# Batch 0 of a block-mixed attention: half of the queries selected early, keys alone on 128 partitions, last values behind the keys

## The chip, the cores and the metric

The kernel runs on one core of a Trainium2 chip. The metric is device time in microseconds (us). The kernel before takes 249.59 us, the median of three runs that lie between 249.53 and 250.57 us.

## The reference

Two steps follow each other. The first is an attention in blocks: batch 4, 8 heads, 768 positions, head size 64, 8 blocks of 96 positions. An 8x8 matrix per head (`sort_net`) goes through five rounds of exponent, row sums and column sums, and then mixes the blocks of keys and of values; each block of queries sees only its own mixed block. The second step is a gated feed-forward on the 3072 tokens of 512 features, with 1536 hidden columns.

```python
P = sort_net
for _ in range(5):
    P = np.exp(P - np.max(P, axis=-1, keepdims=True))
    P = P / (np.sum(P, axis=-1, keepdims=True) + 1e-09)
    P = P / (np.sum(P, axis=-2, keepdims=True) + 1e-09)
k_sb = np.einsum('bhij,bhjcd->bhicd', P, k_b)      # k_b, v_b: (4, 8, 8 blocks, 96, 64)
v_sb = np.einsum('bhij,bhjcd->bhicd', P, v_b)
scores = np.matmul(q_b, k_sb.transpose(0, 1, 2, 4, 3)) / np.sqrt(64)
attn = softmax(scores)
x = np.matmul(attn, v_sb)                          # to (3072 tokens, 512)
g = x @ w_gate                                     # (3072, 1536)
out = (g / (1 + np.exp(-g)) * (x @ w_val)) @ w_out
```

## The kernel before

**Stages.** A prelude computes the mixing weights of all batches on 32 partitions (one per batch and head), five rounds on VectorE with the exponent on ScalarE, while the inputs of batch 0 land. Then the blocks of batch 0 are mixed, the first half of its attention is done (units u = 0 to 3), and the feed-forward begins. It runs in eight pieces `ffn(0)` to `ffn(7)`, each for half a batch (384 tokens); in each, `gate(n, m)` and `value(n, m)` go over the 12 column blocks m of 128. The attention of what comes next is woven between these by hand: `merge` takes a list of feed-forward steps with a rough cost and places side steps at due times on that scale.

**Mixing on TensorE.** A tile of batch 0 holds queries and keys together: `load_q` puts the queries on partitions 64 to 127 (head, block) and `load_k` the keys on 0 to 63, 96 positions of 64 features on each. `kq_chunk(b, at, n, ...)` takes positions at to at+n; for each, two matmuls (`two`, the even and the odd heads) have the tile's slice as weights and `rmix` as the moving operand, 64 columns. `rmix[0]` has the mixing weights on the key rows and an identity on the query rows, so one pass mixes the keys, selects the queries, and puts both with features on partitions. A copy (`drain`) on VectorE ("v") or ScalarE ("s") moves each chunk out of PSUM into `kqt`. `v_chunk` mixes the values: they were first transposed within a partition into `vch` by `copy_v`, partly on GpSimd and partly on ScalarE, and one matmul per feature makes `vt`. A unit is four blocks of one head pair: `qk` (scores and exponent), `av` (values, division into `st`), `xtr` (transposes into `xts`). The four units of the first half each fill one 128-row part of `xts`, which are the four contraction steps of the feed-forward; `early` begins it before all four are there.

**Order.** TensorE, VectorE, ScalarE and GpSimd run in the order written until the first gate outputs; from there TensorE and GpSimd do. `fill` and `dots` are matmuls on zeros that keep TensorE occupied in known gaps.

**Loads.** All input loads are issued by GpSimd on one queue, in this order: values of batch 0 in two halves, queries, keys in four pieces; then GpSimd does its share of `copy_v`, and a one-element copy `landed` (L144), which reads the last key, holds GpSimd until all keys are in. Only behind it come the weights of gate and value, in pieces of 256 columns, with the values of batch 1 among them:

```python
    for m in range(0, 1024, 256):
        load_gv(m, m + 256)          # gate, then value weights, 256 columns each
    load_v(1, 0, C)
    for m in range(1024, DF, 256):
        load_gv(m, m + 256)
```

Column block m of `value` needs the piece that holds columns 128 m to 128 m + 127. PSUM is divided into tags: "gen" (three banks in turn), "a" and "b" (two banks each, one buffer), and "x" (one bank).

Of the kernel before, what the change touches and what calls it, by code (L numbers as in the profile page):

```python
# [17 lines left out]
def kernel(  # L18
# [72 lines left out]
    def load_k(b, lo, hi):  # L91
        rows = highr if b else lowr
        nc.gpsimd.dma_start(out=kq_tile(b)[rows, lo:hi, :], in_=k_nat[b, :, lo:hi, :])
# [6 lines left out]
    def load_q(b, lo, hi):  # L100
        rows = lowr if b else highr
        nc.gpsimd.dma_start(out=kq_tile(b)[rows, lo:hi, :], in_=q_nat[b, :, lo:hi, :])
# [30 lines left out]
    HC = C // 2  # L133
    load_v(0, 0, HC)
    load_v(0, HC, C)
    make_identity(nc, ident)
    load_q(0, 0, C)
    for lo, hi in ((0, 32), (32, 64), (64, 80), (80, 96)):
        load_k(0, lo, hi)
    copy_v(nc.gpsimd, 0, lowr, 0)  # L140
    copy_v(nc.gpsimd, 0, lowr, 3)
    copy_v(nc.gpsimd, 0, lowr, 5, 8, 40, D)
    landed = const.tile([R, 1], BF16)
    nc.gpsimd.tensor_copy(landed, kq_tiles[0][0:R, C - 1, D - 1:D])  # L144
    for m in range(0, 1024, 256):
        load_gv(m, m + 256)
    load_v(1, 0, C)
    for m in range(1024, DF, 256):
        load_gv(m, m + 256)
# [5 lines left out]
    for t in rmix.values():  # L155
        nc.vector.memset(t, 0.0)
# [13 lines left out]
    mask = const.tile([128, H], BF16)  # L170
    id4 = ident.rearrange("p (u h j) -> p h u j", u=2, h=H)
# [9 lines left out]

    p_ps = bank_tile("p_ps")[0:BH, 0:NB * NB].rearrange("p (i j) -> p i j", j=NB)
    for it in range(N_ITER):
        nc.scalar.activation(p_ps, p_sb if it == 0 else p_ps, AF.Exp)
        if it == 1:
            with nc.allow_low_precision("0/1 mask"):
                nc.vector.tensor_reduce(mask, id4, axis=AX.XY, op=ALU.add)
            nc.vector.tensor_copy(rmix[0][highr, 1].rearrange("p h i -> p (h i)"), ident[highr, highr])
        if it == 2:
            copy_v(nc.scalar, 0, lowr, 2, 8)  # L190
        if it == 3:
            copy_v(nc.scalar, 0, lowr, 3, 8)
        rowred = rowreds[it]
        nc.vector.reduce_sum(rowred[:, :, 0], p_ps, axis=AX.X)
        nc.vector.reciprocal(rowred, rowred)
        nc.vector.tensor_mul(p_ps, p_ps, rowred.to_broadcast([BH, NB, NB]))
        nc.vector.reduce_sum(colred[:, 0, :], p_ps.transpose([0, 2, 1]), axis=AX.X)
        nc.vector.reciprocal(colred, colred)
        if it < N_ITER - 1:
            nc.vector.tensor_mul(p_ps, p_ps, colred.to_broadcast([BH, NB, NB]))  # L200
    for lo in (0, NB // 2):
        part = slice(lo, lo + NB // 2)
        nc.vector.tensor_tensor(
            p_bf[:, part], p_ps[:, part].unsqueeze(2).to_broadcast([BH, NB // 2, H, NB]),
            colred.unsqueeze(1).to_broadcast([BH, NB // 2, H, NB]), op=ALU.mult)
    copy_v(nc.scalar, 0, lowr, 4, 8)
    copy_v(nc.scalar, 0, lowr, 5, 8, 0, 40)
# [30 lines left out]
    def v_chunk(b, at, n, eng, tag):  # L238
        rows = slice(0, 128) if b % 2 else lowr
        dst = vt_tile(b // 2)[:, b % 2]  # L240
        mix = rmix[b][rows, 0].rearrange("p a b -> p (a b)")
        tp = chunk_tile("tv", n // 8, tag).rearrange("p (l n) -> p l n", n=H * NB)
        for ld in range(n):
            col = (at + ld) * C
            nc.tensor.matmul(tp[:, ld, :], lhsT=vch[rows, col:col + 128], rhs=mix,  # L245
                             start=True, stop=True)
        drain(eng, dst[:, :, at:at + n], tp[0:C].transpose([0, 2, 1]))

    def v_pair_chunk(pair, at, n, eng, tag):
        dst = vt_tile(pair)[:, :, :, at:at + n]  # L250
# [8 lines left out]

    es, sts, xts = {}, {}, {}  # L260
    ecount = [0]

    def scores(b, u, tag):
        half, g = divmod(u, H2)
# [8 lines left out]
        for i4 in range(4):  # L273
            at = (g * NB + half * 4 + i4) * C
            for two in range(2):
                lo = two * D
                nc.tensor.matmul(pss[two][:, i4 * C:(i4 + 1) * C],  # L277
                                 lhsT=k_sb[lo:lo + D, k_at + at:k_at + at + 128],
                                 rhs=q_sb[lo:lo + D, q_at + at:q_at + at + C],
                                 start=True, stop=True)  # L280
# [15 lines left out]
    def av(b, u, tag="a"):  # L296
        half, g = divmod(u, H2)
# [3 lines left out]
        for two in range(2):  # L301
            e = es[(b, u)][two]
            for i4 in range(4):
                nc.tensor.matmul(o[:, two, i4, :], lhsT=e[:, i4 * C:i4 * C + 128],  # L304
                                 rhs=vt[:, 2 * g + two, half * 4 + i4, :],
                                 start=True, stop=True)
# [105 lines left out]
    idle_ps = bank_tile("idle_ps", "x")  # L412

    def fill(tile, n):
        for _ in range(n):
            nc.tensor.matmul(tile, lhsT=warm_sb[:, 0:128], rhs=warm_sb, start=True, stop=True)  # L416

    def dots(n):
        for _ in range(n):
            nc.tensor.matmul(idle_ps[0:32, 0:32], lhsT=warm_sb[:, 0:32], rhs=warm_sb[:, 0:32],  # L420
                             start=True, stop=True)

    dots(124)
    for it, n in ((1, 3), (2, 4), (3, 4), (4, 4)):
        nc.tensor.matmul(idle_ps[0:NB, 0:NB], lhsT=rowreds[it][:, :, 0], rhs=rowreds[it][:, :, 0],
                         start=True, stop=True)
        fill(idle_ps, n)

    def weights(half):
        w_ps = bank_tile(f"w_ps{half}")[:, 0:NB * B * H].rearrange("p (i b h) -> p i b h", b=B, h=H)  # L430
        for i in range(NB):
            nc.tensor.matmul(w_ps[half * R:(half + 1) * R, i].rearrange("p b h -> p (b h)"),
                             lhsT=p_bf[:, i].rearrange("p a b -> p (a b)"),
                             rhs=ident[0:BH, 0:BH], start=True, stop=True)
        return w_ps

    def mix_of(dst, b, w):
        lo = (b % 2) * R
        nc.vector.tensor_tensor(dst, mask[lo:lo + R].unsqueeze(2).to_broadcast([R, H, NB]),
                                w[lo:lo + R].transpose([0, 2, 1]), op=ALU.mult)  # L440

    w_lo = weights(0)
    mix_of(rmix[0][lowr, 0], 0, w_lo[:, :, 0])
    w_hi = weights(1)
    w_sb = const.tile([128, NB, 2, H], FP32)
    nc.scalar.copy(w_sb[lowr, :, 1], w_lo[lowr, :, 2])
    nc.scalar.copy(w_sb[highr], w_hi[highr].rearrange("p i (pair u) h -> p i pair u h", u=2)[:, :, :, 1])
    fill(idle_ps, 1)
# [4 lines left out]
    v_chunk(0, 48, 8, "v", "gen")  # L453
    v_chunk(0, 56, 8, "s", "gen")
    kq_chunk(0, 0, 8, "v", "gen")
    kq_chunk(0, 8, 16, "s", "a")
    kq_chunk(0, 24, 16, "v", "b")
    kq_chunk(0, 40, 8, "s", "gen")
    kq_chunk(0, 48, 8, "s", "gen")
    fill(idle_ps, 1)  # L460
    kq_chunk(0, 56, 16, "v", "a")
    fill(idle_ps, 1)
    kq_chunk(0, 72, 16, "s", "b")
    kq_chunk(0, 88, 8, "v", "gen")
    for b in range(1, B):
        rows = highr if b % 2 else lowr
        mix_of(rmix["p"][rows, b % 2] if b > 1 else rmix[1][rows, 0], b, w_sb[:, :, b // 2])
    fill(idle_ps, 4)
    qk(0, 0, "a")
    qk(0, 1, "b")  # L470
    qk(0, 2, "gen")
    idle_ps = bank_tile("idle_ps")
    fill(idle_ps, 2)
    av(0, 0, "a")
    fill(idle_ps, 2)
    av(0, 1, "b")
    fill(idle_ps, 1)
    xts[(0, 0)] = xtp.tile([128, H2, TW], BF16, name="xt0_0", tag="xt")
    qk(0, 3, "gen")
    av(0, 2, "a")  # L480
    x01 = xt_tile("x", 2)
    x_to(x01[:, 0], 0, 0)
    x_to(x01[:, 1], 0, 1)
    drain("s", xts[(0, 0)][:, 0:2, :], x01.rearrange("p g a b -> p g (a b)"))
    fill(idle_ps, 1)
    av(0, 3, "b")
    x2 = xt_tile("gen", 1)
    x_to(x2[:, 0], 0, 2)
    drain("s", xts[(0, 0)][:, 2:3, :], x2.rearrange("p g a b -> p g (a b)"))
    first = {}  # L490

    def early(n, kcs):
        sb, m, name = ((wg_sb, 0, "g_ps"), (wv_sb, 0, "v_ps"), (wg_sb, 1, "g_ps"))[n]
        if n not in first:
            first[n] = psum.tile([128, TW], FP32, name=name, tag="gen", bufs=3)
        for kc in kcs:
            nc.tensor.matmul(first[n], lhsT=sb[:, kc, ts(m, 128)], rhs=xts[(0, 0)][:, kc, :],
                             start=(kc == 0), stop=(kc == NKC - 1))

    early(0, (0, 1))  # L500
    early(1, (0, 1))
    x3 = xt_tile("x", 1)
    x_to(x3[:, 0], 0, 3)
    drain("v", xts[(0, 0)][:, 3:4, :], x3.rearrange("p g a b -> p g (a b)"))
    early(0, (2,))
    early(1, (2,))
    early(2, (0,))
    early(0, (3,))
    early(1, (3,))
    early(2, (1, 2, 3))  # L510
# [70 lines left out]
    merge(ffn(0), units(0, range(4, 8), (0.0, 5.6)))  # L581
# [47 lines left out]
```

## Time and profile before

| | us |
|---|---|
| median of three runs | 249.59 |
| the runs | 249.53, 249.59, 250.57 |
| span of the profiled execution | 248.0 |
| TensorE busy in it | 240.1 (97%) |
| VectorE, ScalarE, GpSimd busy | 157.7, 110.3, 52.5 |
| granted TensorE clock | 1.00 throughout |

The profiled execution's own time is given by its span alone, from its first to its last instruction; no separate time is listed for it. The median of the runs is 1.59 us above the span, and that is taken for what lies around it. TensorE's busy time includes the zero matmuls of `fill` and `dots`, and a matmul's end is modelled.

### The profile page before, as it was taken

What the parts mean: (1) busy time and instruction counts of PE and PEld (TensorE: products, weight loads), DVE (VectorE), ACT (ScalarE), POOL (GpSimd) and SP (SyncE); (2) the same over time, 40 slices, a digit from 0 to 9 for tenths busy, and PEclk for the clock granted to TensorE, in tenths of its full rate; (3) what the DMA queues carried; (4) which work ended last, traced back from release to release, by engine and by line L of the source; (5) the groups of instructions that cost most, each with busy time, mean ns of one, the idle gap of its engine ahead of it and who ended that gap; (6) DMA issues with size and microseconds to landing.
All of it is one profiled execution on the core that took longest, in us unless ns stands there. A gap on an engine that the chain in (4) does not pass through costs nothing.

```text
span 248.0 us, 6193 instructions
## 1 busy us (share of the span) xinstructions
PE 240.1 (97%) x2636; PEld 141.3 (57%) x2636; DVE 157.7 (64%) x332; ACT 110.3 (44%) x187; POOL 52.5 (21%) x47
## 2 busy tenths in 40 slices
PE   7899999999999999999999999999999999999994
PEld 6376566666555556655555655565555555555543
DVE  6778689887555775857657646755764585446700
ACT  2977553453544444454642552354244334232311
POOL 7948459960059200000000000000000000000000
PEclk9999999999999999999999999999999999999999
DMA  5959999999999296010122121112111121100122
GB/s 101 211 95 166 215 189 228 194 226 211 221 170 192 53 210 164 3 42 3 45 54 52 57 62 34 44 42 78 32 42 45 39 57 55 42 22 24 42 81 88
DMA packets 39530, 24.38 MB, mean 98 GB/s; under 512 B 27728, under 2 KB 35664, under 8 KB 38992
## 3 DMA queue, kind: packets, MB, share of 16 engines
q0 software_dynamic: 21328, 14.16, 38.9%
q1 hardware_dynamic: 18176, 9.84, 14.1%
q8 instruction: 20, 0.33, 0.5%
q14 instruction: 6, 0.05, 0.1%
HBM read 28.32 MB, written 7.86 MB: 146 GB/s over the span
## 4 chain that ended last, share of the span: by engine, by line
PE 83%; DVE 7%; ACT 3%; issue 3%; DMA 2%; DVEq 0%; ACTq 0%; POOLq 0%
PE v_ps L373 23%; PE o_ps L390 23%; PE g_ps L355 22%; PE tkq L233 4%; PE av_ps L304 3%; PE qk L277 2%; DVE gs_sb L365 2%; DMA v<-in_v_dram 2%; DVE st L310 2%; PE tv L245 2%; PE idle_ps L416 1%; DVE h L378 1%; PE o_ps L406 1%; ACT th_sb L363 1%; PE x_ps L321 1%
## 5 line engine op out<-in xcount | busy, mean ns | idle before, releaser
L365 DVE SCALAR_TENSOR_TENSOR gs_sb<-th_sb,g_ps 128x384 bf16<-128x384 bf16 x96 | 52.8, 550 | 51.8 <-ACT th_sb L363 49.1
L373 PE MATMUL v_ps<-xt,wv_sb 128*128 128x384 bf16 x380 | 77.3, 326 | 0.7 <-DVE gs_sb L365 0.4
L355 PE MATMUL g_ps<-xt,wg_sb 128*128 128x384 bf16 x376 | 76.5, 326 | 0.0
L363 ACT ACTIVATE th_sb<-g_ps 128x384 bf16<-128x384 f32 x96 | 47.1, 490 | 56.0 <-PE g_ps L355 53.5
L390 PE MATMUL o_ps<-wo_sb,h 128*128 128x512 bf16 x276 | 64.0, 379 | 0.0
L378 DVE SCALAR_TENSOR_TENSOR h<-v_ps,gs_sb 128x384 bf16<-128x384 f32 x96 | 53.3, 556 | 6.6
L373 PEld LDWEIGHTS <-wv_sb 128*128 128x128 bf16 x380 | 35.4, 97 | 24.6 <-issue 2.3
L355 PEld LDWEIGHTS <-wg_sb 128*128 128x128 bf16 x376 | 34.6, 97 | 23.2 <-issue 0.3
L390 PEld LDWEIGHTS <-h 128*128 128x128 bf16 x276 | 26.3, 98 | 28.9
L395 ACT COPY o_sb<-o_ps 128x512 f32<-128x512 f32 x23 | 13.5, 585 | 50.8 <-PE o_ps L390 50.8
L124 POOL COPY vch<-v 64x1536 bf16<-64x1536 bf16 (+2 forms) x11 | 28.6, 2639 | 20.7 <-DMA v<-in_v_dram 20.7
L290 ACT ACTIVATE e_all<-qk 96x768 bf16<-96x768 f32 x30 | 22.6, 802 | 8.1 <-PE qk L277 8.1
L310 DVE TENSOR_TENSOR st<-av_ps,r_sb 96x512 bf16<-96x512 f32 x32 | 21.7, 679 | 0.2
L304 PEld LDWEIGHTS <-e_all 96*128 96x128 bf16 x256 | 12.2, 98 | 4.9 <-ACT e_all L290 0.8
L304 PE MATMUL av_ps<-vt,e_all 96*128 96x65 bf16 x256 | 13.5, 194 | 0.0
L211 DVE CAST vt<-tv 96x1024 bf16<-96x1024 f32 (+1 forms) x9 | 9.8, 1100 | 2.7 <-PE tv L255 1.6
L308 DVE RECIPROCAL r_sb<-av_ps 96x8 f32<-96x8 f32 x32 | 6.4, 199 | 7.6 <-PE av_ps L304 7.5
L213 ACT CAST vt<-tv 96x1024 bf16<-96x1024 f32 (+1 forms) x9 | 9.2, 1032 | 3.1 <-PE tv L255 1.8
L211 DVE CAST kqt<-tkq 128x1024 bf16<-128x1024 f32 (+1 forms) x7 | 7.5, 1068 | 2.7 <-PE tkq L233 2.6
L213 ACT CAST kqt<-tkq 128x1024 bf16<-128x1024 f32 (+1 forms) x7 | 6.0, 894 | 6.6 <-PE tkq L233 6.6
L416 PE MATMUL idle_ps<-warm_sb 128*128 128x512 bf16 x28 | 8.7, 409 | 0.0
L233 PE MATMUL tkq<-rmix,kq 128*64 128x64 bf16 x384 | 7.8, 197 | 0.6 <-issue 0.6
(74 smaller groups left out, 126.3 us busy)
## 6 DMA issues: line engine op xcount, KB each, us to landing
out_dram<-o_sb SPq DMA_DIRECT2D x23, 256.0 KB, 2.0
v<-in_v_dram POOLq DMA_DIRECT2D x3, 768.0 KB, 19.9
kq<-in_q_dram POOLq DMA_DIRECT2D x2, 768.0 KB, 13.6
wg_sb<-in_moe_w_gate_dram POOLq DMA_DIRECT2D x6, 256.0 KB, 8.5
wv_sb<-in_moe_w_val_dram POOLq DMA_DIRECT2D x6, 256.0 KB, 9.1
wo_sb<-in_moe_w_out_dram POOLq DMA_DIRECT2D x1, 1536.0 KB, 23.8
kp<-in_k_dram POOLq DMA_DIRECT2D x2, 768.0 KB, 15.1
q_scr<-in_q_dram POOLq DMA_DIRECT2D x2, 768.0 KB, 29.9
```

Of the source, the lines that this page charges most:

```text
L124: eng.tensor_copy(dst, src.transpose([0, 2, 1]))
L211: nc.vector.tensor_copy(dst, src)
L233: nc.tensor.matmul(tp[two * D:(two + 1) * D, lc, :], lhsT=kq_tiles[b][:, at + lc, :], rhs=rm[:, two], start=True, stop=True)
L290: nc.scalar.activation(e_all[:, n:n + 2, 0:4 * C], wide[0:C, :, 0:4 * C], AF.Exp, scale=scale)
L304: nc.tensor.matmul(o[:, two, i4, :], lhsT=e[:, i4 * C:i4 * C + 128], rhs=vt[:, 2 * g + two, half * 4 + i4, :], start=True, stop=True)
L310: nc.vector.tensor_tensor(st.rearrange("p i two d -> p two i d"), o[0:C, :, :, 0:D], r_sb.to_broadcast([C, 2, 4, D]), op=ALU.mult)
L355: nc.tensor.matmul(g_ps, lhsT=wg_sb[:, kc, ts(m, 128)], rhs=xt[:, kc, :], start=(kc == 0), stop=(kc == NKC - 1))
L363: nc.scalar.activation(th_sb, g_ps, AF.Tanh, scale=0.5)
L365: nc.vector.scalar_tensor_tensor(gs_sb, th_sb, 1.0, g_ps, op0=ALU.add, op1=ALU.mult)
L373: nc.tensor.matmul(v_ps, lhsT=wv_sb[:, kc, ts(m, 128)], rhs=xt[:, kc, :], start=(kc == 0), stop=(kc == NKC - 1))
L378: nc.vector.scalar_tensor_tensor(h_tiles[n][:, m, :], v_ps, 0.5, gs_tiles.pop(m), op0=ALU.mult, op1=ALU.mult)
L390: nc.tensor.matmul(o_ps, lhsT=h_w[:, m, ts(t3, 128)], rhs=wo_sb[:, m, :], start=(m == 0), stop=(m == NFC - 1))
```

## The change

The tile of batch 0 becomes `qk0`: keys on all 128 partitions for 48 positions (the first 48 positions of each block on 0 to 63, the last 48 on 64 to 127), and the queries in two quarters of the tile, `q0[0]` and `q0[1]`, one for each half of the sequence. A half is 16 runs of 24 rows, and its partitions are (run, head) with the run outermost. `q0_chunk` selects the first half with the identity ahead of the mixing weights, in the fifth round; the second half, `q0_rest`, is the first side step of `ffn(0)`. `k0_chunk` mixes the keys alone, with a block-diagonal `rmix[0]` that one instruction makes. The last 16 features of the values are mixed behind the keys. Units 0 to 3 of batch 0 are cut differently (two head pairs by two blocks), so that `early` can begin with half of the tokens. The division of `copy_v` over GpSimd and ScalarE changes, the second query half is loaded behind the first weights, the weights from column 512 on come in pieces of 512 columns, and units 4 to 7 are due later in `ffn(0)`.

```diff
+    q_runs = q.rearrange("b h (t r c) d -> b t r h (c d)", t=2, c=QC)          # QC = 24, HC = 48
+    qk0 = natp.tile([128, C, D], BF16, name="qk0", tag="nat")
+    q0 = [qk0[:, HC + t * QC:HC + (t + 1) * QC, :] for t in range(2)]
+    k0 = qk0[:, 0:HC, :]
+    def load_q0(t):
+        nc.gpsimd.dma_start(out=q0[t].rearrange("p c d -> p (c d)"), in_=q_runs[0, t])
     load_v(0, 0, HC)
     load_v(0, HC, C)
     make_identity(nc, ident)
-    load_q(0, 0, C)
-    for lo, hi in ((0, 32), (32, 64), (64, 80), (80, 96)):
-        load_k(0, lo, hi)
-    copy_v(nc.gpsimd, 0, lowr, 0)
-    copy_v(nc.gpsimd, 0, lowr, 3)
-    copy_v(nc.gpsimd, 0, lowr, 5, 8, 40, D)
-    nc.gpsimd.tensor_copy(landed, kq_tiles[0][0:R, C - 1, D - 1:D])
-    for m in range(0, 1024, 256):
-        load_gv(m, m + 256)
+    load_q0(0)
+    for a, rows in enumerate(halves):
+        nc.gpsimd.dma_start(out=k0[rows], in_=k_nat[0, :, a * HC:(a + 1) * HC, :])
+    copy_v0(nc.gpsimd, 0, QC, 0, D3)               # positions, features; D3 = 48
+    copy_v0(nc.gpsimd, HC, C, 0, D3 // 2)
+    copy_v0(nc.gpsimd, HC, C, D3 // 2, D3)
+    copy_v0(nc.gpsimd, HC, C, D3, D)
+    nc.gpsimd.tensor_copy(landed, k0[:, HC - 1, D - 1:D])
+    load_gv(0, 256)
+    load_q0(1)
+    load_gv(256, 512)
+    load_gv(512, 1024)
     load_v(1, 0, C)
-    for m in range(1024, DF, 256):
-        load_gv(m, m + 256)
+    load_gv(1024, DF)
...
+        if 1 < it < 4:
+            copy_v0(nc.scalar, QC + (it - 2) * QC // 2, QC + (it - 1) * QC // 2)
+        if it == 4:
+            early_q = [q0_chunk(0, 0, 16, "b"), q0_chunk(0, 16, 8, "gen")]
+            for dst, src in early_q:
+                drain("s", dst, src)
+            copy_v0(nc.scalar, 0, QC, D3, D)
...
+            fill(idle_ps, (3, 4, 4, 1)[it - 1])    # was 3, 4, 4, 4
...
-    v_chunk(0, 48, 8, "v", "gen")
-    v_chunk(0, 56, 8, "s", "gen")
-    kq_chunk(0, 0, 8, "v", "gen")
...
+    k0_chunk(0, 8, "v", "gen")
+    k0_chunk(8, 8, "s", "gen")
+    k0_chunk(16, 8, "v", "gen")
+    k0_chunk(24, 16, "s", "a")
+    k0_chunk(40, 8, "v", "gen")
+    v_chunk(0, 48, 16, "v", "b")
     fill(idle_ps, 2)
...
+    mix_of(3)
+    x_first(0, "v", "x")                           # 4 transposes, copied out: all features of 2 blocks
+    av(0, 2, "a")
+    x_first(1, "s", "x")
+    early(0, range(NKC), 0)                        # 192 tokens at a time
+    av(0, 3, "b")
+    early(1, range(NKC), 0)
+    x_first(2, "s", "x")
+    early(2, range(NKC), 0)
+    x_first(3, "v", "x")
+    for n in range(3):
+        early(n, range(NKC), 1)
...
-    merge(ffn(0), units(0, range(4, 8), (0.0, 5.6)))
+    def q0_rest():
+        for at, n, eng, tag in ((0, 16, "s", "b"), (16, 8, "v", "a")):
+            drain(eng, *q0_chunk(1, at, n, tag))
+    merge(ffn(0), [(0.0, q0_rest)] + units(0, range(4, 8), (2.0, 6.6)))
```

In the new order `w_ps`, the transposed mixing weights, stays in the "x" bank until `mix_of(3)` has read it, and `x_first` uses the same bank.

## The prediction

> **What bounds the kernel now.** I read the page's busy times first, then the chain of waits in order of time, then the timelines of GpSimd and TensorE, and last the DMA issues with their times to landing. The page says that TensorE is what the time is made of:
>
> ```profile
> PE 240.1 (97%) x2636; PEld 141.3 (57%) x2636; DVE 157.7 (64%) x332; ACT 110.3 (44%) x187; POOL 52.5 (21%) x47
> ```
>
> So a change to the prelude can win in only one way: the feed-forward's matmuls start earlier and then run without a gap. The chain (start, duration, what) gives the fixed points:
>
> ```profile
> 11.28 0.29 PE w_ps L432 x4
> ...
> 20.31 0.62 PE qk L277 x24
> ...
> 27.41 0.65 PE v_ps L373 x4
> ```
>
> The mixing weights start at 11.28, the first scores at 20.31, and 27.41 is the first steady feed-forward step, value(0,1). The prelude is a chain of copies out of PSUM and waits, padded with zero matmuls; from 27.41 on TensorE is dense. Behind it stands the weight queue, in GpSimd's timeline (start, duration, engine, line, what):
>
> ```profile
> 6.30 6.18 POOL L124 COPY vch<-v 64x1536 bf16<-64x1536 bf16 x3 [0.70 <-DMA v<-in_v_dram]
> 15.94 0.18 POOL L144 COPY landed<-kq 64x1 bf16<-64x1 bf16 x1 [3.45 <-DMA kq<-in_k_dram]
> 16.06 0.80 POOL L111 DMA_DIRECT2D wg_sb<-in_moe_w_gate_dram  x1
> ```
>
> GpSimd ends its copies at 12.48, waits for the keys until 15.94, and only then issues weights. In the DMA issues (the last figure is the us from issue to landing) the first piece of gate weights, the first of value weights (issued 16.84) and the last (issued 27.25) stand as
>
> ```profile
> wg_sb<-in_moe_w_gate_dram POOLq DMA_DIRECT2D x1, 256.0 KB, 3.8
> wv_sb<-in_moe_w_val_dram POOLq DMA_DIRECT2D x1, 256.0 KB, 6.0
> wv_sb<-in_moe_w_val_dram POOLq DMA_DIRECT2D x1, 256.0 KB, 13.7
> ```
>
> They land at 19.9, 22.8 and 40.95. TensorE's timeline shows when the late ones are wanted:
>
> ```profile
> 38.48 0.81 PE L355 MATMUL g_ps<-xt,wg_sb 128*128 128x384 bf16 x4
> 39.13 0.81 PE L373 MATMUL v_ps<-xt,wv_sb 128*128 128x384 bf16 x4
> ```
>
> These are gate(0,8) and value(0,8). Their 256-column pieces land at 36.0 and 37.2 (issued 23.09 and 24.52, 12.9 and 12.7 to landing): margins of 2.5 and 1.9 us. value(0,10) needs the last piece at 42.30, margin 1.35. The queue is full from 17.5 to 39.7, as the stretches show (us of the stretch, then PE, PEld, DVE, ACT, POOL, clock, DMA share, GB/s):
>
> ```profile
> 2.60:15.60 13.00, 11.45 (x254) 7.34 (x252) 10.36 (x39) 8.84 (x15) 9.11 (x10) 1.00 0.96 185
> 15.60:17.50 1.90, 1.43 (x63) 1.05 (x56) 1.49 (x2) 1.85 (x3) 1.56 (x3) 1.00 0.00 0
> 17.50:39.70 22.20, 21.86 (x298) 13.49 (x298) 16.91 (x39) 12.50 (x22) 14.94 (x17) 1.00 1.32 192
> ```
>
> So the weights follow TensorE by less than 2 us, and a prelude that is shortened by more runs into them.
>
> **The change: the prelude.** The early selection is 32 and 16 matmuls in the fifth round. In the trace 96 such matmuls took 1.71 us, 18 ns each, so 0.9 us, in place of three fills (0.24 each). Half of the queries is 0.39 MB; at 185 GB/s that is 2.1 us behind the values, whose last part lands near 8, so about 10. TensorE is free from 9.6; 0.9 us of matmuls from 10.0 and one fill end at 11.2, just ahead of 11.28. If they land 1 us later the weights slip by 1 us. Their copies on ScalarE (1.01 and 0.60) and the copy of 384 value elements (0.85, from 1.50 for 768 and 1.01 for 480) end near 12.8, when the first value chunk wants it (12.98 before): hidden. The new `rmix` instruction has 128 columns against 64 (0.21 us): 0.1 more, against one fill taken out.
>
> Behind it VectorE copies 0.69 + 1.22 + 3 x 0.68 of values and keys, ScalarE 0.67 + 1.06 + 0.60 + 1.01; eight key chunks become five, and the last value chunk moves behind them. From 13.0 ScalarE's last key copy, which waits for bank "a" and the matmuls of its chunk, ends at 16.6, so the first scores start at 16.75 instead of 20.31: 3.55 us won.
>
> From there to the steady step the old order took 7.1 us. The new one: first division 1.65 us after the scores (as before), two units of 0.9 on VectorE, then the "x" bank, still held by `w_ps`, comes free only with `mix_of(3)` behind the second unit. x_first(0) copies 0.36; x_first(1) waits for that bank, 0.45; only then four half-width `early` matmuls let av(0,3) pass on TensorE. Division 0.9, two more x_first in the same single bank, 0.8, and twelve 192-token matmuls, 1.0. I get 8.7 us, so the steady step at 25.45: 1.95 won of 3.55. Then `q0_rest`: 48 matmuls, 0.9 us on the path, as TensorE is dense there; 0.3 of it fills the gap before value(0,3) (30.65 to 30.96). Its copies (1.0 on ScalarE, 0.7 on VectorE) hide beside TensorE; VectorE is near full there, and if uncovered they cost up to 0.7. Net 1.4: gate(0,8) and value(0,8) would be ready to run at 37.1 and 37.7.
>
> **The change: the weight queue.** GpSimd now copies 3 x 1152 and 768 elements. By its rows (2.83 us for 1536, 0.65 for 288) that is 3 x 2.16 + 1.49 = 8.0 us, from 6.30 to 14.3. The keys land 2.1 us earlier, near 13.8, so `landed` no longer waits for them but for these copies. Weights are issued from 14.4, 1.65 us earlier. But the second query half, 2.1 us, now stands behind the first pieces. And value(0,8) no longer needs the ninth and tenth of twelve pieces but the whole last one, columns 512 wide.
>
> The last landing is then 40.95 - 1.65 + 2.1 = 41.4 less what wider pieces save. Two 256-column pieces take 2 x 1.35 us by their spacing; the output weights (1024-byte rows also) took 7.0 us between the landing of the queries of batch 1 (48.1) and their own (55.1), 2.35 per third of them, so between 0 and 1.4 us for the four wide pieces: 40.0 to 41.4, 40.5 in the middle. Two irregularities lie in the old 40.95: the second piece landed 3.0 us after the first, and the last 2.4 after the one before it, where 1.35 is usual, 2.7 us too much in sum. Whether they come again the trace can't show: 0 to 2.7 less. I take 1.0 off, since an early dip in the queue is likely again: 39.5. TensorE, ready at 37.7, waits 1.8 us. value(0,8) then starts at 39.5 instead of 39.13: 0.4 later than before, and all behind it moves along, since from there the order and the work are the same.
>
> [...]
>
> **Rivals.** *The queue keeps up.* Without the two irregularities and with the wide pieces at 2.35 us the last one lands near 37.5, before TensorE wants it. Then the whole prelude gain stays: 249.6 - 1.4 = 248.2. For it speaks that the dip at 21 us is not a property of any instruction here; against it, that it needs every term at its better end.
>
> *The last value piece comes late in full.* Same mechanism, worse price: both irregularities again and no gain from width put the landing at 41.4, 2.3 us behind 39.13: 251.8. It decides against the change beyond 0.5% from a landing of 40.4 on. For it: GpSimd's copies may run past 14.3, which moves the queue one to one.
>
> *The early queries don't come early.* If 16 runs outermost do not use all transfer engines, the half takes up to twice 2.1 us, lands near 12, and TensorE holds the mixing weights for 1.5 to 2 us. The keys behind it come later too. Yet the wait for value weights hides up to 1.8 of that: 249.6 to 250.5.
>
> **How the numbers follow.** The profiled span is 248.0; with the 1.59 around it that is the median 249.59. The likeliest case gives +0.4, so 250.0; its own range, with the landing between 38.7 and 40.4, is 249.2 to 250.8. Its chance is 0.48. The queue that keeps up has 0.22; the late piece 0.24; the late queries 0.06, most of it within 0.5%. This kernel's measurement can tell about 0.5% (1.25 us) from no change. Faster by more than that: 0.22; within: 0.50; slower: 0.28. The range 248.1 to 251.6 takes in both rivals but for their ends.
>
> **What would show it.** In the profile after: weights issued on GpSimd near 14.4, with no wait for keys before `landed`; first scores near 16.75; value(0,1) near 25.5; the queries' second half landing near 23; and a gap on TensorE of 1 to 2 us before value(0,8), ended by the DMA of the value weights. If TensorE has no gap there, the sum is wrong by the queue and the time is near 248.2. If the first scores come later than 18, the copies' sum is wrong. If the wait stands ahead of the mixing weights at 11.3, the query load is.

## The result, and the profile after

| | before | after |
|---|---|---|
| median, us (runs) | 249.81 (4: 249.53 to 250.57) | 256.93 (4: 256.64 to 257.24) |
| ratio, 95% interval | | 1.0276 [1.0256, 1.0297] |
| span of the profiled execution, us | 248.0 | 255.3 |
| mean granted TensorE clock | 1.000 | 0.973 |

The change makes the kernel 2.8% slower; 250.0 was predicted, in a range that ended at 251.6. Wherever a run's time and span are both on record, the time is 1.9 to 2.1 us above the span (257.24 against 255.3), not 1.59; this is the same before and after. The mean clock is 0.973 to 0.980 in all four runs after, and 0.998 or more in every run of the kernel before that has one on record, so what the profile shows of the clock is not one run's accident. On the page after, TensorE is still the bound, with more busy time and fewer instructions than before (2636). The second line is the granted clock in 40 slices of 6.4 us, in tenths (9 stands for 0.9 and more; the page before has 9 throughout). The third is the group of the selection matmuls, with its busy time and the mean ns of one:

```profile
PE 242.7 (95%) x2613; PEld 148.4 (58%) x2637; DVE 157.6 (62%) x331; ACT 108.4 (42%) x184; POOL 50.7 (20%) x43
...
PEclk9858799999999999999999999999999999999999
...
L257 PE MATMUL tq<-ident,qk 128*64 128x64 bf16 x96 | 5.9, 295 | 0.9 <-DMA qk<-in_q_dram 0.9
```

96 selection matmuls hold TensorE for 5.9 us; the prediction counted 1.8. TensorE's timeline (start, duration, line, what) places them and the fixed points of the chain:

```profile
10.67 2.97 PE L257 MATMUL tq<-ident,qk 128*64 128x64 bf16 x48 [0.91 <-DMA qk<-in_q_dram]
...
14.23 0.60 PE L474 MATMUL w_ps<-ident,p_bf 32*64 32x32 bf16 x16 [0.47 <-issue]
15.23 2.71 PE L236 MATMUL tv<-rmix,vch 64*128 64x64 bf16 x48 [0.39 <-DVE rmix L477]
17.87 2.77 PE L267 MATMUL tk<-rmix,qk 128*64 128x64 bf16 x96
...
21.91 0.52 PE L337 MATMUL qk<-kqt 64*128 64x96 bf16 x16
...
31.59 0.81 PE L432 MATMUL v_ps<-xt,wv_sb 128*128 128x384 bf16 x4
32.33 2.96 PE L257 MATMUL tq<-ident,qk 128*64 128x64 bf16 x48
35.23 0.82 PE L414 MATMUL g_ps<-xt,wg_sb 128*128 128x384 bf16 x4
```

Both groups of 48 take 2.96 to 2.97 us, 62 ns a matmul. The mixing weights start at 14.23 instead of 11.28, the first scores at 21.91 instead of 20.31, value(0,1) at 31.59 (before 27.24 in the same view; the chain of waits counts it from 27.41). The lines of before in that view:

```profile
12.30 2.04 PE L245 MATMUL tv<-rmix,vch 64*128 64x64 bf16 x64
...
27.24 0.81 PE L373 MATMUL v_ps<-xt,wv_sb 128*128 128x384 bf16 x4
```

So 4.35 us are lost ahead of value(0,1) and 2.96 in the second group: 7.31, and the spans differ by 7.3. The two make up the whole difference.

The stretches show a second cause, the clock (start and end, length, then PE, PEld, DVE, ACT, POOL busy, granted clock, DMA share, GB/s):

```profile
10.60:13.60 3.00, 2.93 (x50) 2.75 (x50) 1.04 (x4) 0.85 (x1) 3.00 (x2) 0.54 0.72 145
...
15.20:18.00 2.80, 2.77 (x53) 2.68 (x53) 1.79 (x3) 0.69 (x2) 2.80 (x6) 0.50 0.37 46
18.00:20.70 2.70, 2.70 (x99) 2.64 (x99) 1.75 (x4) 2.00 (x3) 2.70 (x5) 0.50 1.34 189
...
28.00:31.60 3.60, 3.47 (x29) 2.97 (x27) 1.51 (x4) 0.97 (x2) 0.82 (x1) 0.53 1.28 231
31.60:35.30 3.70, 3.70 (x55) 3.04 (x54) 1.91 (x5) 1.38 (x2) 0.00 (x0) 1.00 0.99 193
```

The clock is 0.50 from 10.87 to 21.11 and from 27.94 to 31.35, 13.65 us in all, where before had none. The value matmuls take 56 ns each there (2.71/48) against 32 before (2.04/64). The second selection group, in the last of the stretches shown, is as slow at clock 1.00 as the first at 0.54: its price is not the clock's.

GpSimd's timeline answers the line on the weight queue:

```profile
9.44 5.85 POOL L154 COPY vch<-v 64x1152 bf16<-64x1152 bf16 x3 [0.82 <-DMA v<-in_v_dram]
15.22 0.19 POOL L162 COPY landed<-qk 128x1 bf16<-128x1 bf16 x1
15.35 0.79 POOL L109 DMA_DIRECT2D wg_sb<-in_moe_w_gate_dram  x1
```

No wait for keys is left ahead of `landed`, as predicted; the weights go out at 15.35 instead of 14.4, since the second copy waited 0.82 us for the second half of the values. The last piece lands at 41.3, where 39.5 was predicted (38.7 to 40.4); but TensorE reaches value(0,8) only at 45.96, so the predicted wait has no place.

### The profile page after: what moved, and what is told of

Read it like the earlier page. It is cut to its first block, busy times and chain, and to the rows that moved or that the text cites. A ratio compares the mean times of both kernels' runs of the same rounds, so it can differ in the third digit from the quotient of the medians.

```text
span 255.3 us, 6166 instructions
## 1 busy us (share of the span) xinstructions
PE 242.7 (95%) x2613; PEld 148.4 (58%) x2637; DVE 157.6 (62%) x331; ACT 108.4 (42%) x184; POOL 50.7 (20%) x43
## 4 chain that ended last, share of the span: by engine, by line
PE 83%; DVE 7%; DMA 3%; issue 3%; ACT 2%; POOL 1%; DVEq 0%; POOLq 0%
PE v_ps L432 22%; PE o_ps L449 22%; PE g_ps L414 22%; DMA qk<-in_q_dram 3%; PE tkq L224 3%; PE av_ps L363 3%; PE tq L257 2%; PE qk L337 2%; PE tv L236 2%; DVE gs_sb L424 2%; DVE st L369 2%; DVE h L437 1%; PE tk L267 1%; PE o_ps L465 1%; PE x_ps L380 1%
## 5 line engine op out<-in xcount | busy, mean ns | idle before, releaser
L449 PE MATMUL o_ps<-wo_sb,h 128*128 128x512 bf16 x255 | 61.5, 379 | 1.3 <-issue 0.3
L122 POOL COPY vch<-v 64x1536 bf16<-64x1536 bf16 (+1 forms) x8 | 22.4, 2850 | 23.2 <-DMA v<-in_v_dram 23.2
L202 DVE CAST vt<-tv 96x1024 bf16<-96x1024 f32 (+1 forms) x9 | 10.4, 1161 | 3.2 <-PE tv L246 1.6
L204 ACT CAST vt<-tv 96x1024 bf16<-96x1024 f32 (+1 forms) x8 | 8.6, 1077 | 4.8 <-PE tv L236 2.9
L154 POOL COPY vch<-v 64x1152 bf16<-64x1152 bf16 (+1 forms) x4 | 8.0, 2025 | 2.7 <-DMA v<-in_v_dram 2.7
L257 PE MATMUL tq<-ident,qk 128*64 128x64 bf16 x96 | 5.9, 295 | 0.9 <-DMA qk<-in_q_dram 0.9
L236 PE MATMUL tv<-rmix,vch 64*128 64x64 bf16 (+1 forms) x128 | 6.1, 213 | 0.4 <-DVE rmix L477 0.4
L257 PEld LDWEIGHTS <-qk 128*64 128x64 bf16 x96 | 5.4, 137 | 1.7 <-DMA qk<-in_q_dram 1.4
```

Of the source, the lines that this page charges most:

```text
L122: eng.tensor_copy(dst, src.transpose([0, 2, 1]))
L257: nc.tensor.matmul(tp[two * D:(two + 1) * D, lc], lhsT=q0[t][:, at + lc, :], rhs=sel[:, two], start=True, stop=True)
L449: nc.tensor.matmul(o_ps, lhsT=h_w[:, m, ts(t3, 128)], rhs=wo_sb[:, m, :], start=(m == 0), stop=(m == NFC - 1))
```

## The experiments

Two theories stood at first. One: the identity is read in steps, `ident` as `p (r g two)` with 8 elements (16 bytes) between neighbours in r, and that makes the selection slow. Two: the clock is what is lost, because zero matmuls were taken out and TensorE waits. The theories can both hold, and do.

**The identity without gaps.**

```diff
+    sel_sb = const.tile([128, 2, R], BF16)
+        if it == 1:
+            nc.vector.tensor_copy(sel_sb.rearrange("p two (g r) -> p two g r", g=H2),
+                                  ident.rearrange("p (r g two) -> p two g r", g=H2, two=2))
-        sel = ident.rearrange("p (r g two) -> p two g r", g=H2, two=2)
+        sel = sel_sb.rearrange("p two (g r) -> p two g r", g=H2)
```

> The changed kernel with one thing more: VectorE copies the identity once into a selection matrix whose columns lie in the order in which the selection matmuls read them, so that these read their moving operand without gaps; before they read it in steps of eight elements. Theory (the read steps cost): each of the two groups of 48 matmuls falls from 2.97 and 2.96 us to about 0.9, the mixing weights start 2.0 us earlier (12.2 instead of 14.23), and the second group, which has TensorE to itself, gives 2.05 more; 256.9 falls to 252.8 if the granted clock is half for as long as before. Rival (the low clock explains the 62 ns per matmul): the second group ran at full clock and stays near 2.96; nothing but noise. Second rival (the slow selection is also what lets the clock down): the half clock from 10.9 to 21.1 goes as well, 251 or less.

Three runs gave 252.25, 252.89 and 254.21, ratio 1.0121 [1.007, 1.0173]. The profiled one took 841 us and is not read: four zero matmuls took 3.32 us in it against 1.04 in the profile before, and its mean clock is given as 1.0; why it was so slow is not known. So the kernel was run again:

> The kernel with the contiguous selection matrix alone once more, since its first profile fell in an execution that took three times as long throughout. To be read in the profile: whether the granted clock still falls to half in the prelude without the slow selection matmuls. If the slow matmuls had let the clock down, it stays at 1.0 and value(0,1) starts near 27; if missing zero matmuls and the wait for the queries do, one or two half-clock windows stay, and value(0,1) starts at 28 to 29.5. Time near 253 either way.

252.76 (251.16 to 255.06, 7 runs), 1.0093 [1.0061, 1.0125]. In its timeline and stretches:

```profile
10.71 0.95 PE L258 MATMUL tq<-sel_sb,qk 128*64 128x64 bf16 x48 [1.14 <-DMA qk<-in_q_dram]
```

```profile
14.94:18.36 3.42, 3.42 (x104) 3.09 (x97) 2.43 (x5) 2.15 (x3) 3.30 (x5) 0.50 0.60 79
```

48 selections take 0.95 us, 20 ns each, as the prediction had them, and this execution, the fastest of the seven, has 3.42 us at half clock instead of 13.65. Its value(0,1) starts at 27.41. So one stretch stays without the slow selection, and the rest goes with it or by chance: the seven runs have mean clocks from 0.980 to 1.000, and one stretch takes off 0.007. By the ratios, 1.8 of the 2.8% are the stepped read: some 4.6 us, of which 4.0 are the matmuls themselves. 0.9% stays, and the 251 of the second rival is not reached.

**Only the second group without gaps.** The same copy, used for the second group alone:

```diff
+        sel = (sel_sb.rearrange("p two (g r) -> p two g r", g=H2) if t else
+               ident.rearrange("p (r g two) -> p two g r", g=H2, two=2))
```

> The changed kernel with the contiguous selection matrix for the second group of 48 matmuls alone, in the feed-forward, where the granted clock is full. Theory (reading the moving operand in steps of eight elements takes 62 instead of 19 ns a matmul): that group falls from 2.96 to 0.95 us and the time by 2.0 us, to 254.9; nothing ahead of it changes. Rival (something else takes the time there, such as the copies it feeds): less than 1 us is won.

254.68 (254.34 to 254.97, 6 runs), 1.0178 [1.015, 1.0207]: 2.2 us less than after. The first group stays at 2.97 us, the second takes 0.95, value(0,1) is nearly where it was (31.27). So what is done in the dense stretch costs the end its full length, and the slow first group, with the clock, keeps most of the loss ahead of value(0,1).

**Which step costs.** The identity copied into tiles with gaps of different width:

```diff
+    sel_sb = [const.tile([128, 2, R, s], BF16, name=f"sel{s}") for s in (2, 4)]    # other kernel: (8, 16)
+        sel = sel_sb[t][:, :, :, 0].rearrange("p two (g r) -> p two g r", g=H2)
```

> The changed kernel with the selection identity copied by VectorE into two tiles: the first group of selection matmuls reads its 64 columns in steps of 2 elements (4 bytes), the second in steps of 4 (8 bytes). Known so far: 62 ns each at steps of 8 elements (16 bytes), 20 ns without gaps. [...] Theory B (the cost grows with the bytes that are passed over): by a straight line from 20 ns at step 1 to 62 at step 8, 26 ns and 38 ns, so 1.2 and 1.8 us for the 48. Theory C (any step other than 1 costs the same): 2.97 us both.

> The same with steps of 8 elements (16 bytes, as in the changed kernel, but read from the copy and not from the identity's own tile) in the first group and of 16 elements (32 bytes) in the second. [...] Theory B (in proportion to the bytes passed over): 2.97 and about 5.2 us (48 x 110 ns, the same line carried to step 16). Theory C (any step): 2.97 both. If the first group takes 0.95 us, it was the identity's tile and not the step that was slow.

The timelines, first of steps 2 and 4, then of 8 and 16:

```profile
11.11 0.95 PE L258 MATMUL tq<-sel,qk 128*64 128x64 bf16 x48 [1.35 <-DMA qk<-in_q_dram]
...
29.72 1.61 PE L258 MATMUL tq<-sel,qk 128*64 128x64 bf16 x48
```

```profile
10.96 2.97 PE L258 MATMUL tq<-sel,qk 128*64 128x64 bf16 x48 [1.40 <-DMA qk<-in_q_dram]
...
31.84 3.00 PE L258 MATMUL tq<-sel,qk 128*64 128x64 bf16 x48
```

A matmul of 64 columns takes 20, 34, 62 and 62 ns at steps of 2, 4, 8 and 16 elements. Neither theory fits: step 2 costs no more than the 20 ns without gaps and 4 costs 34, where any step was to cost 62 (not C); and 16 costs no more than 8, where the straight line has 110 ns (not B). The copy at step 8 takes the same 2.97 us as the identity's own tile, so it is the step that is slow. Measured is a price that rises between steps 2 and 8 and stays at 62 ns at 16; why, these runs do not show. Each width was measured in one execution.

**More zero matmuls.** The change with nine more of them (seven instead of four in the fourth round, six among the first units):

```diff
-            fill(idle_ps, (3, 4, 4, 1)[it - 1])
+            fill(idle_ps, (3, 4, 7, 1)[it - 1])
...
+    fill(idle_ps, 3)            # behind qk(0, 3)
+    fill(idle_ps, 1)            # behind av(0, 2), and 2 behind x_first(1)
```

> The changed kernel with more zero matmuls and nothing else: seven instead of four after the fourth round, while the queries are awaited, and six in the gaps of the first attention units. Theory (the clock is half because TensorE has too little to do in some windows): the half-clock stretches 10.87 to 21.11 and 27.94 to 31.35 shrink or go; v and k matmuls return from 56 and 28 ns to 31 and 18, which is up to 2.5 us in the mixing and about 1 in the early feed-forward: 256.9 falls to between 253.5 and 255.5, and both selection groups stay at 2.9 us. Rival (the slow selection matmuls themselves leave the array idle): the first half-clock stretch stays, and the time stays within 0.5 of 256.9, or is later by the fills.

255.88 (254.67 to 256.1, 4 runs), 1.0222 [1.0183, 1.0261]. The second half-clock stretch is gone and the first shrinks to 6.83 us (15.05 to 21.87), behind the slow selection, which still takes 2.97. This wins about 1 us of 7, less than the theory asked for and more than the rival. The rival has its part: in the 3.41 us ahead of 15.05, over half of them slow selection, TensorE is recorded busy for 3.03, and the clock falls all the same.

**Fewer zero matmuls in the kernel before.** Ten taken out ahead of the first scores, nothing else:

```diff
-((1, 3), (2, 4), (3, 4), (4, 4))
+((1, 3), (2, 4), (3, 4), (4, 1))
-    fill(idle_ps, 1)            # and 1 + 1 among the key chunks, 4 ahead of qk(0, 0)
```

> The kernel before with ten of its zero matmuls taken out: one instead of four after the fifth round, none after the mixing weights, none among the key chunks, none ahead of the first scores. Clock theory: these matmuls hold the granted clock; without them one or two windows of 3.4 us in the prelude are at half clock, and the time rises by 0.5 to 3 us over 249.8. Rival (they only fill gaps): the clock stays at 1.0 and the time is the same or up to 1 us shorter, as four of them stand just ahead of the first scores.

251.07 (249.82 to 251.69, 10 runs), 1.0038 [1.0016, 1.006]. The stretch and the value matmuls:

```profile
11.89:18.71 6.82, 6.70 (x180) 6.50 (x179) 3.87 (x6) 3.99 (x7) 3.53 (x7) 0.50 0.55 97
```

```profile
12.44 3.59 PE L245 MATMUL tv<-rmix,vch 64*128 64x64 bf16 x64
```

The old order too falls to half clock for 6.82 us, and value(0,1) slips by 1.30 (28.54). All ten runs have a mean clock of 0.985 to 0.993, where before has at least 0.998. So the zero matmuls bought the clock, and 6.8 us without it cost 1.3 us there: part of the loss hides in waits.

**Both together.**

> Both edits at once: the contiguous selection matrix and the additional zero matmuls. If read steps and clock are the whole of the loss, the gains add up: 4.1 and up to 3.5 us, 249.3 to 250.3, and what then remains against the sum on record (steady feed-forward at 25.5) is the late query load and a wait for value weights before value(0,8) of up to 1.8 us. If something else holds it back, it stays above 251.

254.39 (251.77 to 256.82, 4 runs), 1.0109 [1.0042, 1.0177], no better than the copy alone. Its timeline tells why:

```profile
11.17 0.95 PE L258 MATMUL tq<-sel_sb,qk 128*64 128x64 bf16 x48 [0.90 <-DMA qk<-in_q_dram]
...
12.50 0.42 PE L478 MATMUL w_ps<-ident,p_bf 32*64 32x32 bf16 x16
...
18.28 0.51 PE L341 MATMUL qk<-kqt 64*128 64x96 bf16 x16
...
26.96 0.81 PE L436 MATMUL v_ps<-xt,wv_sb 128*128 128x384 bf16 x4
...
42.33 1.26 PE L436 MATMUL v_ps<-xt,wv_sb 128*128 128x384 bf16 x4 [2.22 <-DMA wv_sb<-in_moe_w_val_dram]
```

The prelude is at full clock throughout, and now the predicted wait is there: value(0,8) would have been ready at 40.1 and stands for 2.22 us until the last wide piece of value weights is in, at 42.3. (value(0,4) waits 0.45 us for the wide piece before it.) "The identity without gaps" has the same pieces and was ready at 39.9, but its last piece landed at 40.2, and it waited only 0.27:

```profile
40.20 0.82 PE L436 MATMUL v_ps<-xt,wv_sb 128*128 128x384 bf16 x4 [0.27 <-DMA wv_sb<-in_moe_w_val_dram]
```

So the wait's length goes by when the queue delivers, which differs by 2.1 us between these two executions. Behind the 2.22 us the clock is at half for one more stretch, 42.57 to 45.99.

**Weights in narrow pieces.** As the last, with 256 columns in each piece:

```diff
-    load_gv(512, 1024)
+    load_gv(512, 768)
+    load_gv(768, 1024)
-    load_gv(1024, DF)
+    load_gv(1024, 1280)
+    load_gv(1280, DF)
```

> The kernel with the contiguous selection matrix and the additional zero matmuls, and the gate and value weights from column 512 on in pieces of 256 columns again, as in the kernel before. In its wide form TensorE waited 2.2 us at 40.1 for the last value piece, 0.45 us for the one before it, and the granted clock then fell to half for 3.4 us. Theory (wide pieces free their first columns too late): the two waits go or fall below 0.5 us, the clock stays at 1.0 behind them, and 254.4 falls by 3 to 4.5 us to 250 to 251.3. Rival (the queue as a whole is late, whatever the pieces): value(0,8) still waits, less than 1.5 us is won.

251.4 (249.75 to 256.86, 12 runs), 1.0038 [1.0011, 1.0066]. No wait for weights is left in the profiled execution (250.94), whose value(0,1) starts at 27.37, with one half-clock stretch (14.97 to 18.39); value(0,8) starts at once:

```profile
39.73 0.81 PE L438 MATMUL v_ps<-xt,wv_sb 128*128 128x384 bf16 x4
```

The piece that it needs landed at 38.7. That the narrow pieces make the kernel faster than "both" is likely, though the two intervals still overlap.

**The first selection behind the mixing weights.** As the last, with the first group moved behind `w_ps`, its copies one on ScalarE and one on VectorE, and the zero matmuls of the rounds as in the kernel before (four in the fourth and in the fifth, where "narrow weights" has seven and one):

```diff
-            early_q = [q0_chunk(0, 0, 16, "b"), q0_chunk(0, 16, 8, "gen")]
-            for dst, src in early_q:
-                drain("s", dst, src)
+    early_q = [q0_chunk(0, 0, 16, "b"), q0_chunk(0, 16, 8, "gen")]      # behind w_ps
+    drain("s", *early_q[0])
+    drain("v", *early_q[1])
```

> As the kernel with contiguous selection, zero matmuls and 256-column pieces, but the first group of selection matmuls stands behind the mixing weights instead of ahead of them, with one copy on ScalarE and one on VectorE, and the zero matmuls of the five rounds are those of the kernel before. Theory (TensorE holds the mixing weights until the queries are in, 1.2 us): the weights start at 11.3 to 11.5 instead of 12.5, the copies of the queries now stand among those of values and keys and take some of it back; the first scores come 0.5 to 1 us earlier, the time is 0.3 to 1 us below that kernel's, 249.3 to 250.5. Rival (the copies out of PSUM set the pace from there on): the first scores come no earlier, and the time is the same.

251.27 (249.63 to 254.42, 12 runs), 1.0044 [1.0013, 1.0075]. The profiled execution is the one of 249.63: full clock, no wait for weights, value(0,1) at 26.06, which is 1.18 earlier than before; the second group takes 0.95 of it back. That is the whole of what this order wins at its best. Its first scores (17.38) come 0.90 earlier than those of "both" (18.28), also at full clock, but by the ratios it wins nothing over the narrow weights. It was run again, beside a kernel that issues the first weights ahead of GpSimd's last copy:

> The same kernel as e6_queries_behind_weights, once more, to see what a slower execution looks like: its times lay between 249.63 and 254.42, and the profiled one was the fastest. Theory A (half-clock stretches): the span is longer by 1.7 us for each stretch of 3.4 us at half clock, and the work is else as in the first profile. Theory B (late weights): the clock is full, and a wait for gate or value weights of 1 us or more stands in TensorE's timeline before 45 us. If this execution is again near 249.6, nothing is told apart.

250.87 (249.75 to 253.83, 10 runs), 1.0025 [0.9986, 1.0065]. The profiled one took 250.31, again at full clock, with value(0,1) at 25.97 and this behind it:

```profile
42.28 0.82 PE L435 MATMUL v_ps<-xt,wv_sb 128*128 128x384 bf16 x4 [0.50 <-DMA wv_sb<-in_moe_w_val_dram]
```

value(0,10) waits 0.50 us for the last narrow piece, most of the 0.7 between the two executions: a piece of theory B, though under the 1 us that it asked for. No execution above 252 fell on a profile. Theory A does not explain them: 252.88 here and 253.23 before have mean clocks of 1.000 and 0.999, and one stretch at half clock would take off 0.007. What they lose stays open.

```diff
-    copy_v0(nc.gpsimd, HC, C, D3, D)
     landed = const.tile([128, 1], BF16)
     nc.gpsimd.tensor_copy(landed, k0[:, HC - 1, D - 1:D])
     load_gv(0, 256)
+    copy_v0(nc.gpsimd, HC, C, D3, D)
```

> As e6_queries_behind_weights (contiguous selection behind the mixing weights, more zero matmuls, weights in pieces of 256 columns), but GpSimd issues the first gate and value weights ahead of its last copy of values. In e6 its copies end at 14.13 and the weights go out from 14.97; here they should go out near 13.4, 1.6 us earlier, and the last copy ends near 15.9, about when the last value chunk wants it. Theory A (what still limits the mended change is the second query group's 0.95 us and, in some executions, stretches at half clock; the weights are no limit): the median stays within 0.5 us of 251.27, and the profile shows no wait for weights, as in e6. Theory B (in the executions that are slower than the profiled 249.63 the weights come late): the median falls by 1 us or more, to 250.2 or less, and the runs lie closer together than 249.6 to 254.4.

251.8 (251.52 to 252.62, 6 runs), 1.0074 [1.0048, 1.01]. The step failed: with the copy out of the way `landed` waits for the keys until 14.62, the weights go out at 15.09, no earlier, and the last value chunk waits for the copy instead:

```profile
18.16 0.77 PE L239 MATMUL tv<-rmix,vch 64*128 64x64 bf16 x16 [1.80 <-POOL vch L154]
```

So it tells nothing of theory B. None of these versions beats the kernel before.

**The sums.** The table takes the kernels in short names from the paragraphs above. For each profiled execution it gives value(0,1) against 27.24, plus the second selection group, plus later waits for weights, beside the difference of the spans (us):

| kernel | half clock until 35 us | value(0,1) | second group | waits | sum | span less 248.0 |
|---|---|---|---|---|---|---|
| after | 13.7 | +4.35 | 2.96 | | 7.3 | 7.3 |
| more zero matmuls | 6.8 | +3.40 | 2.96 | | 6.4 | 6.2 |
| second group without gaps | 10.2 | +4.03 | 0.95 | 0.2 | 5.2 | 5.0 |
| steps 8 and 16 | 10.2 | +3.85 | 3.00 | | 6.9 | 6.7 |
| steps 2 and 4 | 6.8 | +1.74 | 1.61 | | 3.4 | 3.2 |
| without gaps | 3.4 | +0.17 | 0.95 | 0.3 | 1.4 | 1.2 |
| both | 0 | -0.28 | 0.95 | 2.7 + 1.7 | 5.1 | 5.0 |
| narrow weights | 3.4 | +0.13 | 0.95 | | 1.1 | 0.9 |
| selection behind | 0 | -1.18 | 0.95 | | -0.2 | -0.4 |
| again | 0 | -1.27 | 0.95 | 0.5 | 0.2 | 0.2 |
| weights ahead of the copy | 3.4 | +1.82 | 0.95 | | 2.8 | 2.6 |

The 2.7 are the waits of 0.45 and 2.22, and the 1.7 is an estimate, half of the late half-clock stretch. The sums hold to 0.2 us, so no larger term is missing in these executions. A slow first group and missing zero matmuls both came with more half-clock time (10.2 us in "steps 8 and 16" against 6.8 in "steps 2 and 4"; 13.7 in after against 6.8 in "more zero matmuls"). How much each does is not a fixed number: ahead of value(0,1), "steps 2 and 4" and "without gaps" differ only in the copies of the identity, and their profiled executions have 6.8 and 3.4 us of it; "both" and "narrow weights" have the same work up to the third piece of weights, and one keeps the full clock where the other loses it for 3.4 us. In the first of these pairs the queries landed 0.40 us apart, in the second 0.45.

## Why the prediction was wrong, point by point

*Early queries: 48 matmuls, 0.9 us, ending at 11.2.* This is the step that failed: the price of 18 ns a matmul. It was taken from a row whose moving operand, `rmix`, is read in runs of eight neighbouring elements; these read the identity in steps of 16 bytes and take 62 ns. It costs 2.07 us ahead of the mixing weights and as much again in `q0_rest`. What failed beside it is a missing term, the clock (next point). From the predicted 25.45 to 31.59 value(0,1) slips by 6.1: 2.95 ahead of the mixing weights (14.23 against 11.28), 2.2 from there to the first scores, 1.0 behind them. The queries also landed at 10.67, not 10.0; at 10.7 to 11.2 in the other profiles where TensorE waited for them.

*First scores at 16.75.* They came at 21.91, so by the prediction's own sign the copies' sum would be wrong. It is not: from the mixing weights to the scores 5.47 was predicted, and "both", at full clock with the fast selection, takes 5.78 (12.50 to 18.28). In after it is 7.68, 1.9 more than in "both", because the matmuls run at half clock: those of values and keys take 6.3 us against 4.3. The prediction had no term for the clock: it counted the zero matmuls that were taken out by their own time alone, and put no price on TensorE's wait for the queries beyond the wait itself.

*Scores to value(0,1), 8.7 us.* "Both" and "selection behind" take 8.68. In after it is 9.68, for the half-clock stretch before 31.35.

*`q0_rest`, 0.9 us on the path.* The place was right, since its full length shows at the end; the size was 2.96 for the same reason as the first group, and 0.95 without gaps.

*GpSimd and the weight queue.* Weights at 15.35 instead of 14.4: the sum of copies left out the wait for the values' second half. That no wait for keys was left is partly luck: in "weights ahead of the copy", where `landed` does wait for them, they are in at 14.6, not 13.8. The second query half landed at 24.8 where 23 was predicted, held GpSimd until 25.09, and TensorE did not wait for it. The last piece, at 41.3, came 1.8 later than predicted and near the price of the late-piece rival (41.4): 0.95 of it is the later issue, and the 1.0 that was taken off for the queue's irregularities is about the rest.

*A wait of 1.8 us at value(0,8).* Not in after, where TensorE comes 8.3 us later than predicted (45.96 against 37.7). With the two costs taken away it appears, 2.22 us long in "both" and 0.27 in "without gaps". The mechanism was right, and hidden behind a larger loss; that 2.22 comes so near to 1.8 is luck, since TensorE was ready 2.4 us later than predicted and the piece landed 2.8 later. What the width did the landings show: the wide piece that value(0,8) needs was in at 41.3 in after, 42.3 in "both", 40.2 in "without gaps" and 44.0 in "second group without gaps", the narrow one at 37.2 in before and at 38.7 in "narrow weights".

*The rivals.* None had a price for the selection. "The early queries don't come early" named the right place, ahead of the mixing weights, but its cause, the load, was good for 0.7 us, and it counted on the weight wait to hide the rest.

In one line: predicted -1.95 + 0.6 + 1.8 = +0.4; measured +4.35 + 2.96 + 0 = +7.3. With the selection at its predicted price and most or all of the half-clock time gone, the change comes to +0.25 to +0.44% ("again", "narrow weights" and "selection behind"), inside the 0.5% of the likeliest case, but in kernels that are no longer this change.

## What to carry to other kernels

Take the price of a matmul only from a row whose operands are read in the same way: here an operand rearranged for free in the program cost three times as much at every use (62 ns against 20), and one copy by VectorE bought that back (2.97 us against 0.95 for 48). Zero matmuls that seemed to do nothing also held the clock here (6.82 us at half clock without ten of them, none with them), so a reordering of a prelude is priced with its gaps filled, and the granted clock is the first thing to read in the new profile. The selection work that left the prelude for a dense stretch cost its whole length there, and that took back 0.95 of the 1.18 to 1.27 us that the best order won.

## What the runs showed of the hardware

- Reading the moving operand of a 64-column matmul in steps of 1, 2, 4, 8 and 16 two-byte elements took 20, 20, 34, 62 and 62 ns a matmul; the granted clock, 0.54 or 1.00, made no difference to the 62.
- The clock went to half in stretches of 3.42 us ("both", 42.57 to 45.99), 6.83 ("more zero matmuls", 15.05 to 21.87) and 10.24 (after, 10.87 to 21.11), multiples of 3.41. The busy time of a profile is not what decides: the clock fell behind 3.41 us with 1.64 busy (after, at 10.87), with 2.11 ("fewer zero matmuls", at 11.89) and with 3.03 ("more zero matmuls", at 15.05), and held behind 2.27 (after, 4.05 to 7.46; 1.00 until 10.87). What does decide stays open. One gap of 2.22 us ("both") was followed by 3.42 us at half clock.
- Under half clock TensorE was still "busy": 2.70 of 2.70 us in after's stretch from 18.00. Busy time alone would not have shown it.
